# A fused attention and feed-forward kernel: feed-forward products in slots of one bank, vector work in 128x512 pieces

## The chip, the cores and the metric

The kernel runs on one core of one Trainium2 chip. Its time is the device time of one launch in microseconds (us); lower is better. The engines are TensorE (PE in the profile, its weight loads PEld), VectorE (DVE), ScalarE (ACT), GpSimd (POOL) and SyncE (SP), which issues the DMAs.

## The reference

Clustered attention (16 heads of 768 tokens, 64 wide) gives x, 1536 tokens by 512. Two feed-forward blocks follow, and they are what the change is about:

```python
def _moe_ref(x, w_in, w_out):                 # block 1: 512 -> 2048 -> 512
    h = x @ w_in
    g = np.maximum(h, 0.0) + np.log1p(np.exp(-np.abs(h)))
    return (g @ w_out).astype(np.float32)
...
def _moe2_ref(x, w_gate, w_val, w_out):       # block 2: 512 -> 1536 -> 512
    g = x @ w_gate
    silu = g * (1.0 / (1.0 + np.exp(-g)))
    val = x @ w_val
    return (silu * val @ w_out).astype(np.float32)
```

The feed-forward weights come as float64 and are narrowed to float32 on the chip.

## The kernel before

Every float32 product is made of three products of a faster type, float32r: x = hi + lo, and hi x hi, hi x lo and lo x hi are added up in PSUM. So each operand must be split: `hi` is a cast, `lo` a subtraction. The names end in H or h and L or l (XH, XL; gh, gl; whi, wlo).

Attention runs first; its last three steps, `step(N_IT + 1 + n)`, overlap the first projections, and `fin` scales and splits the last pair of heads into XH and XL.

The feed-forward goes by units of 128 hidden columns, 16 in block 1 and 12 in block 2. Tokens are in three chunks of 512. Everything below is one instruction stream per engine, in the order in which the program writes it; PSUM has eight banks of 128x512, handed out in turn.

- `h_unit` (block 1): three banks, one for each chunk; 36 matmuls (four slices of 128 rows, three products, three chunks; the chunk is the innermost loop, so successive matmuls go to different banks, L731). Then ScalarE takes Abs of each bank (L788), VectorE the maximum with 0 (L789). Over all 1536 tokens at once follow Exp (L792) and Ln (L793) on ScalarE, the sum (L796) on VectorE, the cast to gh (L769) on ScalarE and the subtraction to gl (L770) on GpSimd.
- `y_group` (block 1): for two units, the product with w_out into 12 banks of six matmuls (L813), each added to `acc` by VectorE (L827). Units 2g + 2 and 2g + 3 are projected ahead of group g's products.
- `a_unit` and `o_group` (block 2): gate, Sigmoid (L875), product with the gate (L876), values, product (L887), split; then products with w_out2 (L913), added to acc2 (L925) and, in the last group, sent to memory.
- Weights: each 128x512 tile is loaded as float64 bits, narrowed by one ScalarE instruction (L115) and four VectorE instructions (L116, L119, L123, L126), then split by a cast on VectorE (L135, whi) and a subtraction on GpSimd (L136, wlo). These are tasks in a queue `todo`, two for each tile; `pump` emits one or two of them between parts of the products, and `need` emits tasks until a tile that is asked for is there.

Of the kernel before, what the change touches and what calls it, by code (L numbers as in the profile page):

```python
# [11 lines left out]
F32 = mybir.dt.float32  # L12
F32R = mybir.dt.float32r
# [27 lines left out]
def kernel(  # L41
# [60 lines left out]
    def w_narrow(loaded):  # L102
        """float64 bits [p, a, f, 2] (low word, high word) -> float32 [p, a, f], in two steps

        For 2^-126 <= |x| < 2^128 the float32 exponent is the top bit and the low
        seven bits of the eleven; magnitudes below and above are brought to that
        range's ends first."""
        raw, shape, wide = loaded
        if not wide:
            yield  # L110
            yield raw
# [3 lines left out]
        nc.scalar.activation(out=m.bitcast(F32), in_=hi.bitcast(F32), func=AF.Abs)  # L115
        nc.vector.tensor_scalar(  # L116
# [13 lines left out]

    def w_split(x, pool, tag, bufs):
# [13 lines left out]
    # units of the two feed-forward blocks; a unit's own tiles are split three units  # L145
    # ahead, the tile of the output product with the unit
# [14 lines left out]
    # the first tiles of the second block's values have room early on  # L161
# [11 lines left out]
    W = {}  # L173
# [9 lines left out]
    begun = set()  # L183

    def split_tasks(batch):
        """two steps for each tile"""
# [89 lines left out]
    def warm(n):  # L276
        """the tensor engine's clock rises with its use"""
# [6 lines left out]
    # constants  # L284
# [14 lines left out]
    # centroids over their norms; the block diagonal of a pair of heads  # L299
# [4 lines left out]
    # a square root to float32's accuracy: an estimate and a Newton step  # L304
# [80 lines left out]
    def prep_sims(pr, which, spread=True):  # L385
        """spread: between the transposes of a step"""
# [8 lines left out]
    def prep_arg(pr, step):  # L395
        """the one-hot of the first of the largest"""
# [58 lines left out]
    N_IT = NP * 2 * NT  # L455
    CT = 2                  # query tiles to a chunk of P V
# [124 lines left out]
    # the first pair's; its one-hots get 32 partitions to a head, so that they are copied  # L581
    # to their places by the engines
# [26 lines left out]
    # and the start of the second pair's  # L609
# [93 lines left out]
    for i in range(N_IT + 1):  # L703
# [4 lines left out]
        if i in (0, 26):  # L708
            pump(2)
# [4 lines left out]
    # ================= the two feed-forward blocks =================  # L714
# [10 lines left out]
    def proj(xh, xl, w, banks, kks):  # L725
        """banks[c] += (x @ w)^T over the slices kks, for 512 tokens each"""
        hi, lo = w
        for kk in kks:
            for wt, xt, last in ((hi, xh, 0), (hi, xl, 0), (lo, xh, 1)):
                for c in range(NCH):  # L730
                    nc.tensor.matmul(  # L731
                        banks[c],
                        lhsT=wt[:, kk, :],
                        rhs=xt[:, kk, 512 * c:512 * c + 512],
                        start=(kk == 0 and wt is hi and xt is xh),
                        stop=(kk == KD - 1 and last == 1),
                    )

    # the first products start with the pairs of heads that are done
    h0 = [bank() for _ in range(NCH)]  # L740
    w0 = need(W, ("in", 0))
# [24 lines left out]
    def split_g(g, tag):
        gh = gp.tile([128, NTOK], F32R, tag="gh", name=tag + "h")
        gl = gp.tile([128, NTOK], F32R, tag="gl", name=tag + "l")
        nc.scalar.copy(gh, g)  # L769
        nc.gpsimd.tensor_tensor(out=gl, in0=g, in1=_r(gh), op=ALU.subtract)  # L770
        return gh, gl

    # block 1: y^T = softplus(x w_in) w_out
# [3 lines left out]
    def h_unit(f, banks=None):  # L777
        if banks is None:
            banks = [bank() for _ in range(NCH)]
            w = need(W, ("in", f))  # L780
            for half in range(2):
                proj(XH, XL, w, banks, range(2 * half, 2 * half + 2))
                pump()
        e = tp.tile([128, NTOK], F32, tag="e", name="e")
        r = tp.tile([128, NTOK], F32, tag="s", name="r")
        for c in range(NCH):
            cs = slice(512 * c, 512 * c + 512)
            nc.scalar.activation(out=e[:, cs], in_=banks[c], func=AF.Abs)  # L788
            nc.vector.tensor_scalar_max(r[:, cs], banks[c], 0.0)  # L789

        def log_part():
            nc.scalar.activation(out=e, in_=e, func=AF.Exp, scale=-1.0)  # L792
            nc.scalar.activation(out=e, in_=e, func=AF.Ln, bias=1.0)  # L793

        def sum_part():
            nc.vector.tensor_tensor(out=e, in0=r, in1=e, op=ALU.add)  # L796
            g_t[f] = split_g(e, "g")

        return [log_part, sum_part], split_tasks(batches.pop(0))

    def y_group(g):
        last = g == NF1 // 2 - 1
        nd = 1
        for d0 in range(0, KD, nd):
            banks = [bank() for _ in range(nd * NCH)]
            for ff in range(2):
                hi, lo = need(W, ("out", 2 * g + ff))
                gh, gl = need(g_t, 2 * g + ff)
                for d in range(nd):
                    ds_ = slice(128 * (d0 + d), 128 * (d0 + d) + 128)  # L810
                    for n, (wt, gt) in enumerate(((hi, gh), (hi, gl), (lo, gh))):
                        for c in range(NCH):
                            nc.tensor.matmul(  # L813
                                banks[NCH * d + c],
                                lhsT=wt[:, 0, ds_],
                                rhs=gt[:, 512 * c:512 * c + 512],
# [153 lines left out]
```

## Time and profile before

| | us |
|---|---|
| median of 3 runs | 862.71 |
| lowest and highest | 860.93, 866.04 |
| span of the profiled execution | 861.7 |

The profiled execution's span runs from its first to its last instruction; the page gives no other time for it. TensorE is the busiest engine, 95% of the span. Attention takes the first 260 us or so, block 1 runs to about 560 us, block 2 to the end. A row of the trace names line, engine and operation, then what is written and read; "x3" is a count, and "<-" after idle time names what ended it.

### The profile page before, as it was taken

The numbers are of one execution on the slowest core, as the hardware profiler recorded it, in microseconds if no ns is written. First come the engines' busy times: TensorE is split into PE (matmuls) and PEld (weight loads), VectorE is DVE, ScalarE is ACT, GpSimd is POOL, SyncE is SP. The second block draws the span as 40 slices with busy tenths as digits, with TensorE's granted clock in tenths as the row PEclk, the third lists the DMA queues.
The fourth block names the chain that finished last, engine by engine and source line by source line (L and its number), as shares of the span: only waits on it lengthen the run. The fifth ranks groups of instructions, "written<-read, shape, count | busy, mean of one in ns | idle before, by whom it ended". The sixth has DMA issues, their size and how long they took to land.

```text
span 861.7 us, 11737 instructions
## 1 busy us (share of the span) xinstructions
PE 820.9 (95%) x4366; PEld 697.5 (81%) x4366; DVE 683.9 (79%) x1016; ACT 397.6 (46%) x735; POOL 336.0 (39%) x229
## 2 busy tenths in 40 slices
PE   7999999999999999989898997799999999999998
PEld 6899999999898778768777786588888888888886
DVE  6888978988896778898888888849886868876464
ACT  4689889888893755433244433232212212120210
POOL 3636465555522545444244333424433312332110
PEclk9799999999999999999999999999999999999999
DMA  8975775575312132122221120202312221220003
GB/s 200 248 163 134 190 150 142 141 172 122 85 38 69 49 98 74 51 74 80 65 74 50 49 74 25 68 7 74 97 50 74 74 73 49 74 72 26 1 1 146
DMA packets 65336, 75.42 MB, mean 88 GB/s; under 512 B 28960, under 2 KB 51584, under 8 KB 65280
## 3 DMA queue, kind: packets, MB, share of 16 engines
q1 hardware_dynamic: 65280, 74.68, 32.3%
q8 instruction: 34, 0.56, 0.3%
q14 instruction: 22, 0.18, 0.1%
HBM read 48.27 MB, written 3.19 MB: 60 GB/s over the span
## 4 chain that ended last, share of the span: by engine, by line
PE 60%; DVE 25%; DMA 5%; issue 4%; ACT 4%; POOL 1%; SPq 0%; POOLq 0%; ACTq 0%; DVEq 0%
PE bank L731 28%; PE bank L913 11%; PE sps L466 5%; PE ops L515 5%; DVE m L116 5%; PE tps L498 5%; DVE acc L827 5%; DVE e L796 3%; PE bank L813 2%; DVE r L789 2%; DVE m L126 2%; DVE m L123 2%; DMA rd<-rt 2%; DMA R<-rd 2%; DVE whi L135 2%
## 5 line engine op out<-in xcount | busy, mean ns | idle before, releaser
L136 POOL TENSOR_TENSOR wlo<-m,whi 128x512 fp32r<-128x512 f32 x68 | 100.7, 1480 | 291.9 <-DVE whi L135 266.1
L116 DVE TENSOR_SCALAR m<-m 128x512 f32<-128x512 f32 x68 | 86.0, 1265 | 38.4 <-ACT m L115 38.4
L505 DVE TENSOR_TENSOR tl<-tps,th 128x384 fp32r<-128x384 f32 x192 | 98.8, 550 | 20.2 <-ACT th L504 19.6
L474 DVE TENSOR_REDUCE nm<-sps 128x1 f32<-128x768 f32 x96 | 91.3, 952 | 14.3 <-PE sps L466 11.4
L498 PE MATMUL tps<-id,p 128*128 128x128 f32 x576 | 95.3, 282 | 1.1 <-DVE tl L505 1.1
L504 ACT CAST th<-tps 128x384 fp32r<-128x384 f32 x192 | 84.6, 491 | 20.1 <-PE tps L498 17.1
L482 ACT ACTIVATE p<-sps,nm 128x768 f32<-128x768 f32 x96 | 88.1, 918 | 5.6 <-DVE nm L474 5.6
L466 PE MATMUL sps<-KT,QT 128*128 128x384 f32 x384 | 84.7, 343 | 5.6 <-ACT p L482 3.7
L731 PE MATMUL bank<-YH,whi 128*128 128x512 f32 x288 | 81.6, 391 | 2.5 <-DVE acc L827 2.5
L498 PEld LDWEIGHTS tps<-id,p 128*128 128x128 f32 x576 | 76.4, 153 | 8.4 <-DVE tl L505 5.1
L731 PE MATMUL bank<-YL,whi 128*128 128x512 f32 x288 | 81.6, 392 | 0.0
L731 PE MATMUL bank<-YH,wlo 128*128 128x512 f32 x288 | 81.6, 392 | 0.0
L769 ACT CAST gh<-e 128x1536 fp32r<-128x1536 f32 x16 | 23.7, 1481 | 122.8 <-DVE e L796 122.8
L515 PE MATMUL ops<-th,VV 128*128 128x256 f32 x288 | 79.7, 306 | 0.0
L813 PE MATMUL bank<-gh,whi 128*128 128x512 f32 x192 | 58.9, 407 | 17.3 <-DVE r L789 8.2
L115 ACT ACTIVATE m<-raw 128x512 f32<-128x512 f32 x68 | 44.5, 666 | 62.1 <-POOL wlo L136 62.0
L515 PE MATMUL ops<-tl,VV 128*128 128x256 f32 x288 | 71.9, 279 | 0.0
L770 POOL TENSOR_TENSOR gl<-e,gh 128x1536 fp32r<-128x1536 f32 x16 | 57.1, 3573 | 34.5 <-ACT gh L769 30.7
L466 PEld LDWEIGHTS sps<-KT,QT 128*128 128x128 f32 x384 | 63.4, 191 | 6.7 <-ACT p L482 4.4
L731 PEld LDWEIGHTS bank<-YH,whi 128*128 128x128 f32 x288 | 54.4, 189 | 14.3 <-issue 2.9
L731 PEld LDWEIGHTS bank<-YH,wlo 128*128 128x128 f32 x288 | 54.5, 189 | 11.4
L731 PEld LDWEIGHTS bank<-YL,whi 128*128 128x128 f32 x288 | 54.5, 189 | 11.3
(124 smaller groups left out, 1776.6 us busy)
## 6 DMA issues: line engine op xcount, KB each, us to landing
raw<-in_moe_w_out_dram SPq DMA_DIRECT2D x28, 512.0 KB, 3.3
raw<-in_moe_w_in_dram SPq DMA_DIRECT2D x16, 512.0 KB, 3.9
QT<-hi SPq DMA_DIRECT2D x32, 192.0 KB, 3.1
raw<-in_moe_w_val_dram SPq DMA_DIRECT2D x12, 512.0 KB, 4.0
raw<-in_moe_w_gate_dram SPq DMA_DIRECT2D x12, 512.0 KB, 3.5
KT<-hi SPq DMA_DIRECT2D x14, 384.0 KB, 5.8
qn<-in_q_dram SPq DMA_DIRECT2D x16, 192.0 KB, 5.7
kn<-in_k_dram SPq DMA_DIRECT2D x16, 192.0 KB, 4.2
```

The source lines that it names most:

```text
L116: nc.vector.tensor_scalar(out=m.bitcast(F32), in0=m.bitcast(F32), scalar1=F64_LEAST, scalar2=F64_MOST, op0=ALU.max, op1=ALU.min)
L136: nc.gpsimd.tensor_tensor(out=lo, in0=x, in1=_r(hi), op=ALU.subtract)
L466: nc.tensor.matmul(ps[:, c, 0:384], lhsT=Q[:, a, 128 * j:128 * j + 128], rhs=K[:, a, 384 * c:384 * c + 384], start=(a == 0), stop=(a == 1),)
L474: nc.vector.tensor_reduce(out=nm, in_=ps[:, :, 0:384], axis=AX.XY, op=ALU.max, negate=True)
L482: nc.scalar.activation(out=_h(p), in_=s_t.pop(i)[:, :, 0:384], func=AF.Exp, bias=nm_t.pop(i), accum_out=sm_t[pr][:, j:j + 1],)
L498: nc.tensor.transpose(ps[:, 128 * j:128 * j + 128], p[:, 128 * kb:128 * kb + 128], id32)
L504: nc.scalar.copy(th, pv)
L505: nc.vector.tensor_tensor(out=tl, in0=pv, in1=_r(th), op=ALU.subtract)
L515: nc.tensor.matmul(o[:, 0:CW], lhsT=VV_t[pr][:, hh, kb].rearrange("p a d -> p (a d)"), rhs=t[:, kb, :], start=(kb == 0 and lohi == 0), sto ...
L731: nc.tensor.matmul(banks[c], lhsT=wt[:, kk, :], rhs=xt[:, kk, 512 * c:512 * c + 512], start=(kk == 0 and wt is hi and xt is xh), stop=(kk ...
L813: nc.tensor.matmul(banks[NCH * d + c], lhsT=wt[:, 0, ds_], rhs=gt[:, 512 * c:512 * c + 512], start=(ff == 0 and n == 0), stop=(ff == 1 and ...
L913: nc.tensor.matmul(bk, lhsT=lhs[:, ts_], rhs=rhs[:, 0, :], start=(ff == 0 and n == 0), stop=(ff == 1 and n == 2),)
```

## The change

Block 1 and block 2 are written anew as slots. A projection (`proj`) makes the 12 matmuls of one unit and one chunk, one after the other into one bank. `h_slot` follows it with Abs, Exp and Ln over that bank's 128x512 on ScalarE (`soft`), the maximum and the sum in one VectorE instruction that reads the bank and Ln's result, and, one slot later, the split into gh (ScalarE) and gl (GpSimd), again 128x512 each. `y_group` goes by chunk first and then by output rows. In block 2 a gate slot and a value slot alternate, Silu takes the place of Sigmoid and one product, and output products go in pairs of banks. A small calendar (`soon`, `late`, `tick`) puts the vector work of a slot behind it. Weight tiles are split in four tasks of which the first is free, one task a slot (`pump`); after attention their cast whi is on ScalarE (`cast[0]`). A third weight tile is split within attention, and the first three slots (chunk 0 of units 0, 1 and 2) stand in and after attention's last steps, none behind the first of these.

```diff
-        nc.vector.tensor_copy(hi, x)
+        cast[0](hi, x)
         nc.gpsimd.tensor_tensor(out=lo, in0=x, in1=_r(hi), op=ALU.subtract)
...
-        for _ in range(n or (2 if len(todo) > 4 else 1)):
+    def pump(n=1):
+        for _ in range(n):
             if todo:
+                if todo[0] in firsts:
+                    todo.popleft()()
                 todo.popleft()()
+                if todo and todo[0] in firsts:
+                    todo.popleft()()
...
-        if i in (0, 26):
-            pump(2)
+        if i in (0, 26, N_IT - 14):
+            pump(3)
...
+    def proj(xh, xl, w, c):
+        bk = bank()
         hi, lo = w
+        for kk in range(KD):
+            for n, (wt, xt) in enumerate(((hi, xh), (hi, xl), (lo, xh))):
+                nc.tensor.matmul(
+                    bk,
+                    lhsT=wt[:, kk, :],
+                    rhs=xt[:, kk, 512 * c:512 * c + 512],
...
+    cast[0] = nc.scalar.copy
...
+    def soft(f, c, bk):
+        e = tp.tile([128, 512], F32, tag="e", name="e")
+        nc.scalar.activation(out=e, in_=bk, func=AF.Abs)
+        nc.scalar.activation(out=e, in_=e, func=AF.Exp, scale=-1.0)
+        nc.scalar.activation(out=e, in_=e, func=AF.Ln, bias=1.0)
+        def total():
+            nc.vector.scalar_tensor_tensor(out=e, in0=bk, scalar=0.0, in1=e, op0=ALU.max, op1=ALU.add)
+        late[now[0]].append(total)
+        after(1, late, split_g, g_t, f, c, e)
...
+    def h_slot(f, c, n=1):
+        if (f, c) not in hb:
+            hb[f, c] = proj(XH, XL, need(W, ("in", f)), c)
+        after(1, soon, soft, f, c, hb.pop((f, c)))
+        if c == NCH - 1:
+            todo.extend(split_tasks(batches.pop(0)))
+        tick(n)
...
+            nc.scalar.activation(out=sg, in_=bk, func=AF.Silu)
...
+    def o_group(g):
+        for t0 in range(0, NTOK // 128, 2):
...
+            for t, bk in enumerate(bks, t0):
+                after(1, soon, o_sum, g, t, bk)
+            tick()
```

VectorE in the middle of block 1. Before, from one sum over 1536 tokens (L796) to the next:

```order
L796 TENSOR_TENSOR e<-r,e 128x1536
L116 TENSOR_SCALAR m<-m 128x512 [waits Activation_49]
L119 TENSOR_SCALAR m<-m 128x512 [waits DVE_49]
L827 TENSOR_TENSOR acc<-bank,acc 128x512 [waits PE_49] x3
L123 SCALAR_TENSOR_TENSOR m<-raw,m 128x512 [waits DMAHW2_49,DVE_49]
L126 SCALAR_TENSOR_TENSOR m<-raw,m 128x512 [waits DVE_49]
L135 CAST whi<-m 128x512 [waits DVE_49]
```

Now, where the sums into acc end and the slots begin (L812 is the fused maximum and sum, L118 to L128 the weight steps L116 to L126):

```order
L830 TENSOR_TENSOR acc<-bank,acc 128x512
L118 TENSOR_SCALAR m<-m 128x512 [waits Activation_49]
L121 TENSOR_SCALAR m<-m 128x512 [waits DVE_49]
L812 SCALAR_TENSOR_TENSOR e<-bank,e 128x512 [waits Activation_49]
L125 SCALAR_TENSOR_TENSOR m<-raw,m 128x512 [waits DMAHW0_49,DVE_49]
L128 SCALAR_TENSOR_TENSOR m<-raw,m 128x512 [waits DVE_49]
L812 SCALAR_TENSOR_TENSOR e<-bank,e 128x512 [waits Activation_49] x2
```

The cast is gone from VectorE, the maximum and the sum have become L812, and a weight tile's steps stand between pieces of one slot.

TensorE at attention's end (ops are attention's last products, L515 before). Before, three banks in turn behind the first of the last steps:

```order
L515 MATMUL ops<-tl,VV 128x256
L731 MATMUL bank<-XH,whi 128x512 x3
L731 MATMUL bank<-XL,whi 128x512 x3
L731 MATMUL bank<-XH,wlo 128x512 x3
L515 MATMUL ops<-th,VV 128x256 [waits DVE_49]
```

Now, with the tiles' numbers, the same place:

```order
L526 MATMUL ops_3877<-tl_3807,VV_3225 128x256
L526 MATMUL ops_3921<-th_3863,VV_3225 128x256
L526 MATMUL ops_3921<-tl_3864,VV_3225 128x256
L526 MATMUL ops_3921<-th_3863,VV_3225 128x256
L526 MATMUL ops_3921<-tl_3864,VV_3225 128x256
L526 MATMUL ops_3921<-th_3863,VV_3225 128x256
L526 MATMUL ops_3921<-tl_3864,VV_3225 128x256
L742 MATMUL bank_3928<-XH_65,whi_342 128x512
L742 MATMUL bank_3928<-XL_66,whi_342 128x512
L742 MATMUL bank_3928<-XH_65,wlo_343 128x512
L742 MATMUL bank_3928<-XH_65,whi_342 128x512
```

The second group of ops follows the first with no projection between them, and the projection that comes then stays in one bank.

ScalarE around the start of an output group in block 1. Before, late in the block, with the weights' first step L115 as the only step of a weight tile:

```order
L788 ACTIVATE e<-bank 128x512 [waits PE_49] x3
L792 ACTIVATE e<-e 128x1536 [waits Activation_49]
L793 ACTIVATE e<-e 128x1536 [waits Activation_49]
L115 ACTIVATE m<-raw 128x512 [waits DMAHW1_49,Pool_49]
L788 ACTIVATE e<-bank 128x512 [waits PE_49,Pool_49]
```

Now, from the last slot of unit 11 on (L807 to L809 are its Abs, Exp and Ln, L798 the copies gh, L140 the cast whi, L116 the next tile's first step); the first L140 is that of w_out's tile 9, for which the fifth output group asks:

```order
L807 ACTIVATE e<-bank 128x512 [waits PE_49,Pool_49]
L808 ACTIVATE e<-e 128x512 [waits Activation_49]
L809 ACTIVATE e<-e 128x512 [waits Activation_49]
L798 CAST gh<-e 128x512 [waits DVE_49]
L140 CAST whi<-m 128x512 [waits DVE_49]
L116 ACTIVATE m<-raw 128x512 [waits DMAHW6_49,Pool_49]
L798 CAST gh<-e 128x512
```

The cast whi now stands on ScalarE behind a slot's three functions and a copy.

## Rows read from the trace of the kernel before

**Rows 1.** The page's busy times, share of the span, instructions.

```profile
PE 820.9 (95%) x4366; PEld 697.5 (81%) x4366; DVE 683.9 (79%) x1016; ACT 397.6 (46%) x735; POOL 336.0 (39%) x229
```

**Rows 2.** Busy time by engine, two stretches: PE, PEld, DVE, ACT, POOL, PEclk, DMA, GB/s.

```profile
260.00:560.00 300.00, 275.81 (x1174) 220.05 (x1174) 252.81 (x333) 127.11 (x157) 121.94 (x57) 0.99 0.21 64
560.00:860.00 300.00, 297.86 (x1294) 243.65 (x1293) 213.36 (x305) 59.75 (x87) 83.13 (x45) 0.99 0.18 59
```

**Rows 3.** Who TensorE waited for, 259 to 560 us: total, times, longest.

```profile
PE bank L813 <- DVE r L789: 8.2, 5, 3.8
PE bank L813 <- DVE acc L827: 7.9, 5, 2.4
```

**Rows 4.** In order of time near 415 us: start, us, engine, instruction, idle before.

```profile
414.40 3.50 POOL L770 TENSOR_TENSOR gl<-e,gh 128x1536 fp32r<-128x1536 f32 x1 [5.40 <-ACT gh L769]
...
414.91 3.27 DVE L116 TENSOR_SCALAR m<-m 128x512 f32<-128x512 f32 x1 [2.10 <-ACT m L115]
...
419.30 0.60 PE L813 MATMUL bank<-gh,whi 128*128 128x512 f32 x1 [2.39 <-DVE acc L827]
```

**Rows 5.** Busy time by engine, one stretch; the granted clock is 0.93.

```profile
420.00:440.00 20.00, 20.00 (x83) 16.36 (x83) 17.55 (x24) 6.84 (x8) 8.87 (x4) 0.93 0.25 80
```

**Rows 6.** Single lines, 260 to 862 us: duration in ns, least/median/most, first, last.

```profile
L116 DVE TENSOR_SCALAR m<-m x66: 412/420/3346, 270.5 to 832.2; 128x512 f32<-128x512 f32 x66
...
L119 DVE TENSOR_SCALAR m<-m x66: 426/428/3614, 271.0 to 832.6; 128x512 int32<-128x512 int32 x66
...
L126 DVE SCALAR_TENSOR_TENSOR m<-raw,m x66: 691/692/1670, 272.2 to 836.8; 128x512 int32<-128x512 int32 x66
...
L136 POOL TENSOR_TENSOR wlo<-m,whi x66: 1269/1303/2663, 273.4 to 838.2; 128x512 fp32r<-128x512 f32 x66
```

**Rows 7.** Groups by line, 260 to 560 us: busy, mean ns of one; idle before.

```profile
L136 POOL TENSOR_TENSOR wlo<-m,whi 128x512 fp32r<-128x512 f32 x36 | 58.4, 1621 | 138.1 <-DVE whi L135 120.6 <-PE bank L813 14.6 <-PE bank L731 2.9
...
L770 POOL TENSOR_TENSOR gl<-e,gh 128x1536 fp32r<-128x1536 f32 x16 | 57.1, 3573 | 34.5 <-ACT gh L769 30.7 <-issue 3.8
...
L116 DVE TENSOR_SCALAR m<-m 128x512 f32<-128x512 f32 x36 | 53.1, 1476 | 27.5 <-ACT m L115 27.5
...
L827 DVE TENSOR_TENSOR acc<-bank,acc 128x512 f32<-128x512 f32 x79 | 49.6, 679 | 0.2 <-PE bank L813 0.2
...
L789 DVE TENSOR_SCALAR r<-bank 128x512 f32<-128x512 f32 x48 | 30.0, 680 | 6.1 <-ACT e L788 6.1
...
L796 DVE TENSOR_TENSOR e<-r,e 128x1536 f32<-128x1536 f32 x16 | 29.0, 1817 | 0.1
...
L788 ACT ACTIVATE e<-bank 128x512 f32<-128x512 f32 x48 | 25.0, 595 | 10.8 <-PE bank L731 9.0 <-POOL gl L770 1.9
...
L115 ACT ACTIVATE m<-raw 128x512 f32<-128x512 f32 x36 | 23.5, 665 | 7.6 <-POOL wlo L136 7.6
...
L829 ACT CAST YH<-acc 128x512 fp32r<-128x512 f32 x7 | 4.3, 621 | 21.7 <-DVE acc L827 21.7
```

**Rows 8.** The chain that ended last: start, us, engine, line, count.

```profile
266.32 20.43 PE bank L731 x90
...
403.34 3.75 PE bank L813 x16
...
559.62 66.66 PE bank L731 x286
...
626.28 16.81 PE bank L913 x72
...
855.80 2.79 DVE acc L925 x4
```

**Rows 9.** In order of time, attention's end: start, us, engine, instruction, idle before.

```profile
260.33 1.02 DVE L505 TENSOR_TENSOR tl<-tps,th 128x384 fp32r<-128x384 f32 x2 [0.57 <-ACT th L504]
...
260.65 0.84 PE L731 MATMUL bank<-XH,whi 128*128 128x512 f32 x3
...
269.41 0.51 ACT L577 CAST XH<-xu 128x384 fp32r<-128x384 f32 x1 [1.09 <-DVE xu L575]
```

More of the change, by code (lines that the diff above doesn't have):

```diff
@@ L129, in w_narrow @@
         yield m.bitcast(F32)
+    cast = [nc.vector.tensor_copy]
     def w_split(x, pool, tag, bufs):
@@ L723, in bank, with tick, after @@
         return pool.tile([128, 512], F32, tag="b", name="bank")
-    def proj(xh, xl, w, banks, kks):
+    def proj(xh, xl, w, c):
+        bk = bank()
         hi, lo = w
[L728 to L741, printed above, removed]
+        for kk in range(KD):
[4 more added lines that the diff above has]
+                    rhs=xt[:, kk, 512 * c:512 * c + 512],
+                    start=(kk == 0 and n == 0),
+                    stop=(kk == KD - 1 and n == 2),
+                )
+        return bk
+    cast[0] = nc.scalar.copy
+    soon, late = collections.defaultdict(list), collections.defaultdict(list)
+    now = [0]
+    def tick(n=1):
+        now[0] += 1
+        for f in soon.pop(now[0], []):
+            f()
+        pump(n)
+        for f in late.pop(now[0], []):
+            f()
+    def after(lag, table, f, *a):
+        table[now[0] + lag].append(functools.partial(f, *a))
+    hb = {}
     for n in range(3):
         step(N_IT + 1 + n)
-        proj(XH, XL, w0, h0, range(n, n + 1))
+        if n:
+            hb[n - 1, 0] = proj(XH, XL, need(W, ("in", n - 1)), 0)
     assert not events, events
+    hb[2, 0] = proj(XH, XL, need(W, ("in", 2)), 0)
     pctx.close()
@@ L762, with cols @@
     gp = ctx.enter_context(tc.tile_pool(name="gp", bufs=4, reuse_waits="tile"))
-    tp = ctx.enter_context(tc.tile_pool(name="tp", bufs=2, reuse_waits="tile"))
+    tp = ctx.enter_context(tc.tile_pool(name="tp", bufs=4, reuse_waits="tile"))
     pool_of["c"] = (mp, 3)
[L766 to L771, printed above, removed]
+    def cols(c):
+        return slice(512 * c, 512 * c + 512)
@@ L774, with split_g @@
+    def split_g(table, f, c, g):
+        if f not in table:
+            table[f] = [gp.tile([128, NTOK], F32R, tag=t, name=t) for t in ("gh", "gl")]
+        gh, gl = table[f]
+        nc.scalar.copy(gh[:, cols(c)], g)
+        nc.gpsimd.tensor_tensor(out=gl[:, cols(c)], in0=g, in1=_r(gh)[:, cols(c)], op=ALU.subtract)
     acc = mp.tile([128, KD, NTOK], F32, tag="acc", name="acc")
     g_t = {}
[L777 to L799, printed above, removed]
@@ L801, in y_group, with y_sum @@
+    def y_sum(g, d, c, bk):
+        a = acc[:, d, cols(c)]
+        if g == 0:
+            nc.scalar.copy(a, bk)
+        else:
+            nc.vector.tensor_tensor(out=a, in0=bk, in1=a, op=ALU.add)
+        if g == NF1 // 2 - 1:
+            nc.scalar.copy(YH[:, d, cols(c)], a)
+            eng = nc.gpsimd if c < NCH - 1 else nc.vector
+            eng.tensor_tensor(out=YL[:, d, cols(c)], in0=a, in1=_r(YH)[:, d, cols(c)], op=ALU.subtract)
     def y_group(g):
-        last = g == NF1 // 2 - 1
@@ L803, in y_group @@
-        nd = 1
-        for d0 in range(0, KD, nd):
-            banks = [bank() for _ in range(nd * NCH)]
+        for n in range(KD * NCH):
+            c, d = divmod(n, KD)
+            bk = bank()
             for ff in range(2):
                 hi, lo = need(W, ("out", 2 * g + ff))
[L808 to L816, printed above, removed]
-                                start=(ff == 0 and n == 0),
-                                stop=(ff == 1 and n == 2),
-                            )
-            for n, bk in enumerate(banks):
-                d, c = d0 + n // NCH, n % NCH
-                cs = slice(512 * c, 512 * c + 512)
-                a = acc[:, d, cs]
-                if g == 0:
-                    nc.scalar.copy(a, bk)
-                else:
-                    nc.vector.tensor_tensor(out=a, in0=bk, in1=a, op=ALU.add)
-                if last:
-                    nc.scalar.copy(YH[:, d, cs], a)
-                    eng = nc.gpsimd if c == 1 or c == 2 and d < KD - 1 else nc.vector
-                    eng.tensor_tensor(out=YL[:, d, cs], in0=a, in1=_r(YH)[:, d, cs], op=ALU.subtract)
-            pump()
@@ new lines, in a_slots, with silu, product @@
+    def a_slots(f, c):
+        bk = proj(YH, YL, need(W, ("gate", f)), c)
+        sg = tp.tile([128, 512], F32, tag="e", name="sg")
+        def silu(bk=bk):
+            nc.scalar.activation(out=sg, in_=bk, func=AF.Silu)
+        after(1, soon, silu)
+        tick()
+        bk = proj(YH, YL, need(W, ("val", f)), c)
+        def product():
+            nc.vector.tensor_tensor(out=sg, in0=bk, in1=sg, op=ALU.mult)
+            after(1, soon, split_g, a_t, f, c, sg)
+        after(1, soon, product)
+        if c == NCH - 1 and batches:
+            todo.extend(split_tasks(batches.pop(0)))
+        tick()
@@ L904, in o_group, with o_sum @@
+    def o_sum(g, t, bk):
+        a = acc2[:, t, :]
+        if g == 0:
+            nc.vector.tensor_copy(a, bk)
+        else:
+            nc.vector.tensor_tensor(out=a, in0=bk, in1=a, op=ALU.add)
+        if g == NF2 // 2 - 1:
+            nc.sync.dma_start(out=outv[t // NT, t % NT], in_=a)
     def o_group(g):
-        for t0 in range(0, NTOK // 128, 4):
-            bks = [bank() for _ in range(4)]
+        for t0 in range(0, NTOK // 128, 2):
+            bks = [bank() for _ in range(2)]
```

139 lines of the change are left out of this document (48 added, 91 removed).

## The prediction

> **What bounds the kernel now.** I read the busy shares first, then the two blocks of the feed-forward by windows, then who TensorE waited for, then one such wait in order of time. TensorE is busy 95% of the span [rows 1], but not evenly: between 260 and 560 us, block 1 (softplus), it is busy 275.81 of 300 us, between 560 and 860 us, block 2, 297.86 [rows 2]. So block 2 is bound by its matmuls, and what the change does to vector work there is worth nothing unless it makes TensorE wait; block 1 has 24.2 us of waits. The longest are for VectorE, for the maximum (L789) and the sum into acc (L827), which empty the banks [rows 3]. [rows 4] show one: GpSimd's 128x1536 subtraction gl (L770) begins at 414.40 and takes 3.50 us; VectorE's L116 begins at 414.91 and ends 0.3 us behind it, after 3.27 us, where its median is 0.420 [rows 6]. The bank sums stand behind it on VectorE, and TensorE waits 2.39 us. Over 420 to 440 us the granted clock is then 0.93 [rows 5], so for a part of that stretch the lower level (1.2 GHz): 0.07 x 20 = 1.4 us for such a drop. VectorE is busy 252.81 of 300 us [rows 2], of which L116 has 53.1 where 36 x 0.420 = 15.1 would do [rows 6, 7]: 38.0 us are spent blocked.
>
> The Trainium skill (SBUF — State Buffer, section Who interferes with whom) says that GpSimd and a VectorE instruction in a two-port mode exclude each other for a whole instruction; L116 agrees. It says the same of VectorE instructions with two SBUF inputs, which would make L126 a victim too; L126's median is 0.692 and its longest 1.670, so here this happens seldom.
>
> **The floor of block 1.** It has 576 projection matmuls and 576 output matmuls. Unhindered one takes 20.43 / 90 = 0.227 and 3.75 / 16 = 0.234 us [rows 8]: 130.8 + 134.8 = 265.6 us. From the first projection at 260.65 [rows 9] to block 2's first at 559.62 [rows 8] it takes 299.0 now.
>
> **VectorE in block 1, for a unit of 128 hidden columns.** Now: two weight tiles of 0.420 + 0.428 + 0.692 (the unshown L123 taken as L126, same shape) + 0.692 and the cast (taken as L119, 0.428), 5.3; six sums of 0.679, 4.1; three maxima of 0.680 and one sum of 1.817, 3.9 [rows 6, 7]; 38.0 / 16 = 2.4 of blocking: 15.7 of TensorE's 265.6 / 16 = 16.6, with waits on top. After: the cast goes to ScalarE, -0.9. The fused step has one PSUM and one SBUF operand like L827, so 3 x 0.68 = 2.0 for the 3.9. That leaves 10.6. The blocking lies between 0 and all of GpSimd's work, five 128x512 pieces a unit of 1.303 (L136) = 6.5 us; I take the share of now, 38.0 of the 58.4 + 57.1 us that L136 and L770 ran, a third: 2.1, in all 12.7. VectorE no longer sets the pace, and one block lasts 1.3 us, not 3.5.
>
> **ScalarE in block 1.** Abs 0.595, and Exp, Ln and the copy gh 0.621 each (L829, the same shape) make 2.46 a slot; a weight tile 0.665 + 0.621 for the new cast = 1.29 [rows 7]. A unit: 3 x 2.46 + 2 x 1.29 = 10.0 of 16.6. Within the six slots of a pair of units it is 14.8 + 2.6 = 17.4 against 72 x 0.227 = 16.3 for TensorE; eight banks cover the lag of 1.1, and in the 12 output banks that follow (16.8 us, two tiles or 2.6 of ScalarE) it is made up.
>
> **Where TensorE will still wait.** (1) The first of attention's last three steps has no projection behind it now; the next needs tl, begun at 260.33 and 1.02 long [rows 9]: 0.8 us. Those steps' own matmuls cost 1.4, as before. (2) The first output group. ScalarE turns to the slots after its last copy to XH, at 269.9 [rows 9]: 12 x 1.84 + 11 copies x 0.62 + 6.5 tiles x 1.29 = 37.3, so to 307.2, the fused step behind it to 307.9. The eighth output bank reuses the twelfth slot's, and TensorE is there at 260.65 + 0.8 + 1.4 + 12 x 2.72 + 7 x 1.40 = 305.4: 2.5, ends 0 and 5. (3) Two weight tiles, w_out's 9 and 15, aren't finished when the output product asks. For tile 9 the order on ScalarE shows it: behind the three functions of unit 11's last slot stands a copy gh and only then the cast whi; on GpSimd gl stands before wlo. From the end of that slot: 1.84 + 0.62 + 0.62 = 3.1 to whi, asked for at 0.7: 2.4; wlo at 2.5 + 2 x 1.3 = 5.1, asked for at 3.1 + 0.5: 1.5. Together 3.9. For tile 15 VectorE's four steps, 2.2, stand behind a sum of 0.7, then 0.62 and 1.3, so whi at 3.5 and wlo at 4.8: 2.8 + 0.8, or 3.7 unrounded. (4) Each of these two lets the clock drop: 2 x 1.4 = 2.8.
>
> Sum: 265.6 + 1.4 + 0.8 + 2.5 + 3.9 + 3.7 + 2.8 = 280.7, which is 18.3 under 299.0. The step to block 2 costs nothing: the last output group goes by chunks of tokens, so 8 banks (11 us) lie between the last sum of chunk 0 and the gate slot that reads it; without that cover a sum, a copy and a subtraction would stand there, 0.68 + 0.62 + 1.3 = 2.6.
>
> **Small terms.** A third weight tile within attention: VectorE 2.7 with its cast, of which I take 0.5 (ends 0 and 2.7). The end: two banks are finished together there, so two sums of 2.79 / 4 = 0.7 [rows 8] stand behind the last matmul, the first begun a matmul early, where one stood: +0.4. Silu, the dropped product, the smaller pieces, the paired banks in block 2: nothing, under its matmuls; VectorE has 300 - 213.36 = 87 us to spare there [rows 2], and only past that would they cost. The program has as many table loads as before. The weights' loads keep their number and their three buffers, at a DMA share of 0.21 [rows 2].
>
> **Twelve matmuls to one bank.** The trace has no projection that adds twelve times to one bank. In L913 two of three successions stay in a bank, at 16.81 / 72 = 0.2335; L813 changes it every time and takes 0.234 [rows 8]. So the 7 ns over 0.227 go with the operands, not with the bank, and I take 0.227. The ends: the output products sink to 0.227 too, 1008 x 6.5 ns = -6.6; the projections rise to 0.2335, 1440 x 6.5 ns = +9.4.
>
> **The sum.** 861.7 - 18.3 + 0.5 + 0.4 = 844.3 us of span. The median of the runs, 862.71, is 1.0 above the span of before: **845.3 us**. Half a per cent, 4.3 us, is what a measurement of this kernel can tell from no change.
>
> **Rivals.** (A) The forecast, 838 to 852 by the ends of its terms: 0.58. (B) No waits: the 12.9 us of (2) to (4) go, 832.4: 0.10. For it: eight banks, three spare tiles; against it: the order at tile 9. (C) The vector engines still set the pace in block 1: VectorE is blocked for all of GpSimd's 6.5, 10.6 + 6.5 = 17.1 a unit, (17.1 - 16.6) x 16 = 8 us more, 853.3; with ScalarE's 1.1 in each of six pairs not made up, 859.9: 0.16, of which 0.03 for the latter. The skill's rule on two SBUF inputs would bring this case, as GpSimd's pieces are more now; L126's median speaks against. (D) The other side: successive additions to one bank delay each other. Its place is the 1440 projections, its price 1.44 us for each ns. At 0.2335 a matmul it gives 854.7 (0.05); from (17.4 + 4.3) / 1440 = 15 ns on, 0.242 a matmul, the kernel is slower than before, 871.2 at 0.245 (0.07); between them 0.04. For it: no run of twelve is in the trace; against it: L913. That the work doesn't keep a slot behind, as the change says, is (3), and counted.
>
> **Chances.** Faster by over 0.5%: 0.58 + 0.10 + 0.13 + 0.05 = 0.86; within: 0.03 + 0.04 = 0.07; slower: 0.07. The range 832 to 858 leaves out C's upper end and D's upper two cases.
>
> **What would show it.** Block 1: its stretch from the first projection to block 2's first gate lasts 281 us; L116 (now L118) means under 0.9 us and never over 1.8; TensorE waits about 4 us twice, for a cast whi and a subtraction wlo, and nowhere over 1 us for acc. Projections keep 0.227; more means D. If the fused step or ScalarE ends a wait of TensorE in most pairs, it is C. If block 2 takes over 300 us, its cover is gone and I am wrong there.

## The result and the profile after

The changed kernel takes 872.17 us (median of 4 runs, 870.06 to 875.1) and the kernel before, on the same chip, 863.38 (860.93 to 866.04). The ratio is 1.010, 95% interval 1.0072 to 1.0129: **slower by 1%**, where 845.3 was predicted. The profiled execution takes 872.08 us, its span is 870.3.

The busy line of the page of after, which answers to [rows 1]:

```profile
PE 825.1 (95%) x4366; PEld 702.2 (81%) x4366; DVE 566.7 (65%) x895; ACT 458.6 (53%) x918; POOL 345.2 (40%) x287
```

VectorE is relieved as meant, from 79% to 65%, and TensorE is as busy as before, 95%, in a longer span. The chain that ended last of after (start, us, what), as [rows 8]:

```profile
271.20 2.72 PE bank L742 x12
...
332.48 16.33 PE bank L742 x72
348.81 16.86 PE bank L845 x72
...
569.14 65.28 PE bank L742 x288
```

The timeline shows the first projection (the chain has it 0.2 us later):

```profile
268.89 0.28 PE L526 MATMUL ops<-tl,VV 128*128 128x256 f32 x1
270.22 0.39 PE L526 MATMUL ops<-th,VV 128*128 128x256 f32 x1 [1.05 <-DVE xu L547]
...
271.03 0.39 PE L742 MATMUL bank<-XH,whi 128*128 128x512 f32 x1
```

It comes at 271.03 where it came at 260.65 [rows 9], 10.4 us later. But it also stands one step of attention later in the order than before: the 2.0 us from 269.0 on, a wait of 1.05 us and the matmuls of that step, lie ahead of it now, and the prediction counts them in block 1. So attention itself has lost 8.4 us. From its first projection block 1 takes 298 us up to block 2's first gate at 569.14; with the 2.0 us it is 300, where it took 299.0: the 18.3 us that were to be gained there are not there. Block 2 lasts as long as before, 301.2 to the end against 302.1, and TensorE waits for nothing in it. What TensorE waited for in after (us in total, times, longest), to be held against [rows 3]:

```profile
PE bank L845 <- ACT whi L140: 11.2, 3, 5.8
PE sps L477 <- ACT p L493: 10.1, 2, 9.0
PE bank L742 <- ACT whi L140: 4.5, 1, 4.5
PE bank L845 <- DVE e L812: 3.0, 1, 3.0
PE tps L509 <- DVE tl L516: 2.7, 4, 1.3
...
PE bank L845 <- POOL wlo L141: 0.8, 2, 0.6
```

The waits for sums and maxima of [rows 3] are gone. In block 1 TensorE now waits for weight tiles: 11.2 + 4.5 + 0.8 us, with the 3.0 for the first output group 19.5. In attention its longest wait is 9.0 us, for the exponential (p). And the clock falls oftener; the windows of after in block 1 whose granted clock is under 0.95 (busy times of PE, PEld, DVE, ACT, POOL, then the granted clock, DMA share, GB/s), as [rows 5]:

```profile
300.00:320.00 20.00, 18.98 (x70) 14.80 (x71) 14.83 (x20) 14.21 (x25) 10.36 (x8) 0.83 0.29 85
...
440.00:460.00 20.00, 14.03 (x52) 10.66 (x51) 12.62 (x13) 13.39 (x24) 11.89 (x9) 0.84 0.17 52
...
480.00:500.00 20.00, 17.50 (x69) 13.65 (x69) 11.08 (x15) 14.14 (x25) 10.45 (x8) 0.91 0.17 52
...
540.00:560.00 20.00, 16.28 (x57) 12.22 (x56) 12.36 (x22) 4.23 (x7) 5.77 (x5) 0.83 0.18 54
```

20 x (0.17 + 0.16 + 0.09 + 0.17) = 11.8 us, at most: the clock can fall shortly before a wait ends, and that part costs nothing. Floor 265.6 + the last step's matmuls 0.7 + waits 19.5 + clock 11.8 = 297.6 accounts for block 1's 298.

**Two of these waits in order of time.** The timeline of after where TensorE asks for the weight tile of w_in's unit 3, called in 3 here (start, us, engine, line; in brackets the idle time before and what ended it):

```profile
295.68 0.63 ACT L809 ACTIVATE e<-e 128x512 f32<-128x512 f32 x1
296.22 0.64 ACT L116 ACTIVATE m<-raw 128x512 f32<-128x512 f32 x1
296.89 0.43 DVE L118 TENSOR_SCALAR m<-m 128x512 f32<-128x512 f32 x1 [2.12 <-ACT m L116]
...
297.82 1.64 DVE L125 SCALAR_TENSOR_TENSOR m<-raw,m 128x512 int32<-128x512 int32 x1
...
300.21 0.62 ACT L140 CAST whi<-m 128x512 fp32r<-128x512 f32 x1 [1.03 <-DVE m L128]
...
300.88 0.80 PE L742 MATMUL bank<-XH,whi 128*128 128x512 f32 x1 [4.49 <-ACT whi L140]
```

TensorE ran out at 296.4, and the tile's first step (Abs, L116) began at 296.22, behind a softplus function on ScalarE; VectorE had been idle 2.12 us for it. And w_out's tile 9, out 9:

```profile
448.50 0.66 ACT L116 ACTIVATE m<-raw 128x512 f32<-128x512 f32 x1
448.74 1.28 POOL L141 TENSOR_TENSOR wlo<-m,whi 128x512 fp32r<-128x512 f32 x1 [1.15 <-ACT whi L140]
...
449.19 1.11 DVE L118 TENSOR_SCALAR m<-m 128x512 f32<-128x512 f32 x1 [0.31 <-ACT m L116]
...
449.98 1.45 POOL L799 TENSOR_TENSOR gl<-e,gh 128x512 fp32r<-128x512 f32 x1
...
450.34 1.38 DVE L121 TENSOR_SCALAR m<-m 128x512 int32<-128x512 int32 x1
...
452.07 1.26 POOL L799 TENSOR_TENSOR gl<-e,gh 128x512 fp32r<-128x512 f32 x1 [0.64 <-ACT gh L798]
452.24 1.64 DVE L125 SCALAR_TENSOR_TENSOR m<-raw,m 128x512 int32<-128x512 int32 x1
453.92 0.69 DVE L128 SCALAR_TENSOR_TENSOR m<-raw,m 128x512 int32<-128x512 int32 x1
454.64 0.62 ACT L140 CAST whi<-m 128x512 fp32r<-128x512 f32 x1 [2.65 <-DVE m L128]
```

The whole tile is made within the 6.8 us before its use (PE follows at 455.31, after 5.83 us). Three of VectorE's four steps take 1.11, 1.38 and 1.64 us where unblocked ones take 0.43, 0.43 and 0.68: each overlaps a piece of GpSimd, wlo (L141) or gl (L799). So a tile seems to be late because its steps are handed out late, at one task a slot, and most of them then take long; the runs below test that.

**Attention's start.** The timeline of after where the 9.0 us wait ends:

```profile
26.93 0.66 ACT L116 ACTIVATE m<-raw 128x512 f32<-128x512 f32 x1 [8.32 <-DMA raw<-in_moe_w_in_dram]
27.62 0.90 ACT L493 ACTIVATE p<-sps,nm 128x768 f32<-128x768 f32 x1
...
28.66 1.65 PE L477 MATMUL sps<-KT,QT 128*128 128x384 f32 x4 [8.95 <-ACT p L493]
```

At step 0 the new `pump` hands out a tile's three tasks and then also the next tile's free first one. That one is an Abs on ScalarE, whose data come by DMA only at 26.9; attention's exponential stands behind it, and TensorE behind that.

### The profile page after: what moved, and what is told of

The parts are those of the page before. It is cut to its first block, busy times and chain, and to the rows that moved or that the text cites. A ratio compares the mean times of both kernels' runs of the same rounds, so it can differ in the third digit from the quotient of the medians.

```text
span 870.3 us, 11899 instructions
## 1 busy us (share of the span) xinstructions
PE 825.1 (95%) x4366; PEld 702.2 (81%) x4366; DVE 566.7 (65%) x895; ACT 458.6 (53%) x918; POOL 345.2 (40%) x287
## 4 chain that ended last, share of the span: by engine, by line
PE 78%; ACT 7%; DVE 7%; DMA 3%; issue 2%; SPq 1%; POOL 1%; DVEq 0%; POOLq 0%; ACTq 0%
PE bank L742 31%; PE bank L845 15%; PE bank L910 12%; PE tps L509 6%; PE ops L526 6%; PE sps L477 6%; PE sims L388 2%; ACT e L808 1%; DVE m L125 1%; ACT e L807 1%; DVE tl L516 1%; DVE m L118 1%; PE mps L351 1%; DVE m L128 1%; DMA R<-rd 1%
## 5 line engine op out<-in xcount | busy, mean ns | idle before, releaser
L141 POOL TENSOR_TENSOR wlo<-m,whi 128x512 fp32r<-128x512 f32 x68 | 88.0, 1294 | 232.5 <-ACT whi L140 150.2
L742 PE MATMUL bank<-YL,whi 128*128 128x512 f32 x288 | 112.1, 389 | 0.0
L742 PE MATMUL bank<-YH,whi 128*128 128x512 f32 x288 | 112.1, 389 | 0.0
L140 ACT CAST whi<-m 128x512 fp32r<-128x512 f32 x65 | 40.0, 616 | 136.7 <-DVE m L128 136.7
L516 DVE TENSOR_TENSOR tl<-tps,th 128x384 fp32r<-128x384 f32 x192 | 99.0, 551 | 18.9 <-ACT th L515 18.5
L485 DVE TENSOR_REDUCE nm<-sps 128x1 f32<-128x768 f32 x96 | 91.5, 953 | 21.3 <-PE sps L477 18.7
L515 ACT CAST th<-tps 128x384 fp32r<-128x384 f32 x192 | 85.0, 492 | 23.2 <-PE tps L509 20.3
L845 PE MATMUL bank<-gh,whi 128*128 128x512 f32 x192 | 79.3, 413 | 14.2 <-ACT whi L140 11.2
L799 POOL TENSOR_TENSOR gl<-sg,gh 128x512 fp32r<-128x512 f32 x36 | 50.9, 1415 | 94.5 <-ACT gh L798 94.5
L799 POOL TENSOR_TENSOR gl<-e,gh 128x512 fp32r<-128x512 f32 x48 | 67.6, 1413 | 33.3 <-ACT gh L798 23.1
L742 PE MATMUL bank<-XH,whi 128*128 128x512 f32 x192 | 76.0, 396 | 4.5 <-ACT whi L140 4.5
L845 PE MATMUL bank<-gh,wlo 128*128 128x512 f32 x192 | 79.0, 411 | 1.0 <-POOL wlo L141 0.8
L830 DVE TENSOR_TENSOR acc<-bank,acc 128x512 f32<-128x512 f32 x84 | 55.9, 685 | 36.2 <-PE bank L845 36.1
L845 PE MATMUL bank<-gl,whi 128*128 128x512 f32 x192 | 78.3, 408 | 0.0
L742 PE MATMUL bank<-XH,wlo 128*128 128x512 f32 x192 | 75.8, 395 | 0.1
```

The costliest lines, as they stand in the source:

```text
L485: nc.vector.tensor_reduce(out=nm, in_=ps[:, :, 0:384], axis=AX.XY, op=ALU.max, negate=True)
L515: nc.scalar.copy(th, pv)
L516: nc.vector.tensor_tensor(out=tl, in0=pv, in1=_r(th), op=ALU.subtract)
L742: nc.tensor.matmul(bk, lhsT=wt[:, kk, :], rhs=xt[:, kk, 512 * c:512 * c + 512], start=(kk == 0 and n == 0), stop=(kk == KD - 1 and n == 2),)
L799: nc.gpsimd.tensor_tensor(out=gl[:, cols(c)], in0=g, in1=_r(gh)[:, cols(c)], op=ALU.subtract)
L845: nc.tensor.matmul(bk, lhsT=wt[:, 0, ds_], rhs=gt[:, cols(c)], start=(ff == 0 and j == 0), stop=(ff == 1 and j == 2),)
```

## The experiments

My theory: (a) the early Abs costs attention some 6 us; (b) late tiles cost block 1 the rest. The rivals stand with each run. A row gives the median, the ratio to the kernel before on the same chip with its interval, and, by the chain of the profile, attention's end (start of the first projection) and block 1 (from there to block 2's first gate, in the kernel before behind its wait of 2.5 us). In before, e3 and e4 the first projection stands a step of attention earlier: against the other rows add 2.0 to their attention's end and take 2.0 from their block 1.

| run | median us | ratio | attention's end | block 1 |
|---|---|---|---|---|
| before | 863.38 | 1 | 260.8 | 298.8 |
| after | 872.17 | 1.010 [1.0072, 1.0129] | 271.2 | 297.9 |
| e1_no_front_abs | 867.55 | 1.0044 [1.0029, 1.0059] | 265.8 | 298.9 |
| e2_tiles_early | 853.08 | 0.9867 [0.9828, 0.9907] | 273.9 | 278.2 |
| e3_before_front_abs | 870.92 | 1.0085 [1.0063, 1.0107] | 266.3 | 300.2 |
| e4_before_gl3 | 854.44 | 0.9896 [0.9867, 0.9926] | 263.9 | 290.9 |
| e5_spread | 868.38 | 1.0054 [1.0032, 1.0076] | 264.2 | 299.9 |
| e6_spread_tiles | 847.77 | 0.9808 [0.9772, 0.9843] | 265.7 | 279.0 |
| e7_order | 849.05 | 0.9829 [0.98, 0.9859] | 270.3 | 278.8 |
| e8_cast_on_vector | 864.74 | 0.9999 [0.9982, 1.0015] | 272.3 | 289.3 |
| e9_rest_on_vector | 868.07 | 1.0057 [1.0027, 1.0088] | 274.7 | 292.3 |
| e10_tiles_and_cast | 842.67 | 0.976 [0.973, 0.979] | 267.9 | 274.8 |
| e11_tiles_cast_order | 845.25 | 0.9803 [0.9784, 0.9822] | 266.5 | 275.3 |
| e12_tiles_cast_rest | 845.75 | 0.9811 [0.9772, 0.985] | 269.0 | 277.9 |

### No early Abs, and the early Abs alone

```diff
 # e1, on after
-            pump(3)
+            for _ in range(4):
+                todo.popleft()()
 # e3, on before
-            pump(2)
+            pump(3 if i == 0 else 1)
```

> The changed kernel, but within attention each of the three weight tiles is split in exactly four tasks, without the Abs of the following tile that the new pump emits behind them. Theory T1 (ScalarE's Abs stands ahead of attention's first exponential and waits there for its tile's load): the 9.0 us wait of TensorE near 20 us goes, the later loss near 235 us stays: 872.2 - 6 = 866. Rival R1 (the whole tile in one burst, or the third tile, is what delays attention): no change, 871 to 873.

> The kernel before, with one thing of the change alone: at attention's first step the Abs of the second weight tile is emitted behind the first tile's two tasks. T1: 863.4 + 6 = 869, and ScalarE waits some 8 us for the load of raw ahead of the first exponential. R1: no change, 862 to 865.

Both ways it is the Abs: taking it away (e1, at all three tiles) gains 4.6 us, and putting it alone into the kernel before (e3, at the first) costs 7.4. TensorE's waits for the exponential, first in e1, then in e3:

```profile
PE sps L477 <- ACT p L493: 2.4, 2, 1.4
```

```profile
PE sps L466 <- ACT p L482: 9.4, 2, 8.5
```

### Tiles handed out earlier

```diff
 # e2, on after: y_group
-                tick()
+                tick(2)
```

> The changed kernel, but two weight-tile tasks instead of one in every slot of the first block's output products, so that no tile is unfinished when it is asked for. Theory T2 (TensorE's waits in block 1 are tiles that come too late, each followed by a stretch at the lower clock): the waits near 450, 492 and 546 us go, 5.8 + 2.5 + 3.7 = 12.0, and 8.5 us of lower clock with them: 872.2 - 20 = 852; the waits near 296 and 322 us stay. Rival R2 (ScalarE, VectorE and GpSimd together are too slow for block 1, so that the waits only move): 869 to 875.

19 us for one figure. The same instructions are issued; only the tasks come earlier in the order. What is left of TensorE's waits in block 1 in e2, but for one of 0.4 us:

```profile
PE bank L742 <- ACT whi L140: 4.5, 1, 4.5
PE bank L845 <- DVE e L812: 3.2, 1, 3.2
```

The 11.2 us for w_out's tiles are gone, and with them all clock drops of block 1 but the one after in 3. The wait for in 3 lies before the first output group, where nothing was changed, and stays at 4.5. Of the 19.7 us by which block 1 is shorter, 11.4 are waits and some 8.4 go with the clock, which falls once now (3.4 us) where it fell four times.

### The pieces alone, in the kernel before

```diff
 # e4, on before
-        nc.gpsimd.tensor_tensor(out=gl, in0=g, in1=_r(gh), op=ALU.subtract)
+        for c in range(NCH):
+            cs = slice(512 * c, 512 * c + 512)
+            nc.gpsimd.tensor_tensor(out=gl[:, cs], in0=g[:, cs], in1=_r(gh)[:, cs], op=ALU.subtract)
```

> The kernel before, with GpSimd's subtraction gl of block 1 in three pieces of 128x512 and nothing else. Theory T3 (one 3.5 us subtraction that holds VectorE's L116 is what makes TensorE wait in the kernel before): L116 is never over 1.8 us, TensorE's waits in block 1 fall from 24 to some 12 us, 863.4 - 10 = 853. Rival R3 (the blocking is GpSimd's total time, which only grows, and VectorE's own work sets the pace): within 3 us of 863.

So the reading of [rows 4] was right: GpSimd's long subtraction made the bank sums late, and cutting it in three is worth 1% by itself. In block 1 L116's longest falls from 3.29 to 1.58 us, and block 1 from 298.8 to 290.9.

### The third tile spread over attention

```diff
 # e5, on after
-        if i in (0, 26, N_IT - 14):
-            pump(3)
+        if i in (0, 26):
+            for _ in range(4):
+                todo.popleft()()
+        if i in (42, 48, 54, 60):
+            todo.popleft()()
 # e6: and tick(2) in y_group
```

> The changed kernel; in attention the tasks of a tile are handed out so that no free first is pulled ahead at step 0, and the third tile's four tasks go one at a time to steps 42, 48, 54 and 60 in place of all at step 82. Theory: attention's loss against the kernel before (10.4 us) is these two bursts, so nearly all but the new tail (about 1 us) comes back: 872.2 less 8 to 9 = 863 to 864, with the first projection near 262. Rival: the third tile costs VectorE's place in attention wherever it stands; then as in the run without the early free first, 867.5.

> The same, and in the feed-forward's output groups two tasks are handed out at a step instead of one, so that the weight tiles are finished earlier. Theory: the two losses lie in different stages and add: 853.1 less 8 to 9 = 844 to 845, which is the prediction's own floor with its clock drops. Rival: block 1 starting earlier finds its tiles as much later, and the gains don't add: 850 or more.

e5 is no faster than e1 (1.0054 against 1.0044): my theory of two bursts falls by half. Spread out, the third tile brings TensorE 5.3 us of waits for tl (L516) where after has 2.7. VectorE has little room in attention: 16.5 to 18.7 us busy of each 20 from 60 us on. In e1 the tile's burst is followed by a wait of 2.3 us for tl and a stretch with the clock at 0.57 (230 to 238 us), which e5 does not have. What the tile costs is not shown. By e1's profile the first projection comes 265.6 - 260.65 = 4.9 later than before, of which 2.0 are its later place in the order: 2.9 for the tile; by e5's it would be 1.4. And e4, whose attention is that of the kernel before, ends it 3.1 us later than that kernel's profile. A version without the third tile was not tried. e6 lies 5.3 below e2, as e1 lies 4.6 below after: the two losses add, but to 848, not to the 844 that I expected of all of attention's loss.

### Another order of the first slots

```diff
 # e7, on e6
-    for f, c in ((0, 0), (1, 0), (2, 0), (0, 1), (1, 1), (0, 2), (1, 2), ...
+    for f, c in ((0, 0), (1, 0), (2, 0), (0, 1), (0, 2), (1, 1), (1, 2), ...
```

> The same, and the first slots of block 1 run in an order that ends with a weight tile one slot earlier, so that the tile in 3 gets its buffers earlier. Theory: the wait for in 3 (4.5 us in the run with two tasks a step) is a wait for buffers and falls by about one slot's 2.7 us, and the clock drop behind it (up to 3.4 us) with it: 839 to 842. Rival: the tile is late because VectorE and GpSimd can't make it faster: no change against the run before this one, 845.

The time is the rival's, but its reason is not: the wait for in 3 does fall, from 4.5 to 2.3, only the time doesn't. TensorE's waits in e7, and its windows:

```profile
PE bank L848 <- DVE e L815: 4.1, 1, 4.1
PE bank L745 <- ACT whi L140: 2.3, 1, 2.3
```

```profile
290.00:310.00 20.00, 17.60 (x64) 13.48 (x63) 11.65 (x16) 17.43 (x31) 11.95 (x9) 0.83 0.22 70
310.00:330.00 20.00, 15.89 (x60) 12.40 (x59) 16.46 (x19) 12.52 (x23) 10.75 (x8) 0.83 0.29 90
```

The next wait grew by 0.5 (3.6 in e6), I take it because ScalarE is late by the same work, which no run separates; and the clock falls twice by 0.17 x 20 = 3.4 us, where in e6 the second fall cost 1.8 (0.91 in the same window). The shorter wait cost a whole fall all the same.

### The cast of weight tiles back on VectorE

```diff
 # e8, on after
-    cast[0] = nc.scalar.copy
 # e9, on e8: wlo on VectorE too, from block 1 on
-        nc.gpsimd.tensor_tensor(out=lo, in0=x, in1=_r(hi), op=ALU.subtract)
+        rest[0].tensor_tensor(out=lo, in0=x, in1=_r(hi), op=ALU.subtract)
```

> The changed kernel with the last cast of a weight tile left on VectorE after attention, in place of ScalarE. Theory: tiles are late because their VectorE steps are handed out late, and the cast's engine matters by no more than its queue: within 3 us of 872.2. Rival: the cast waits in ScalarE's queue behind the softplus functions and makes the tiles late: 5 us or more faster.

> The changed kernel with both the weight cast and the weight rest (the subtraction that makes wlo) on VectorE from block 1 on, in place of ScalarE and GpSimd. To be held against the run with the cast alone on VectorE, 864.7. Theory: VectorE's steps of a late tile are slow because GpSimd's pieces block them (out 9's two last steps took 1.69 us instead of 0.68), and wlo is the smaller half of GpSimd's work in block 1 (35 pieces of 1.29 against 48 of 1.41 us); with it gone, and with wlo 0.6 us shorter, tiles are finished earlier: 858 to 862. Rival: VectorE pays 0.69 us for each wlo and stays blocked by the other pieces: 863 to 868.

Here my theory fell: e8 is 7.4 us faster than after, so the cast's engine matters too. The timeline of e8 at in 3:

```profile
295.19 0.64 ACT L116 ACTIVATE m<-raw 128x512 f32<-128x512 f32 x1
...
299.69 0.42 DVE L140 CAST whi<-m 128x512 fp32r<-128x512 f32 x1
...
300.17 0.50 PE L742 MATMUL bank<-XH,whi 128*128 128x512 f32 x1 [2.62 <-DVE whi L140]
```

TensorE ran out at 297.55 here and the Abs began 2.36 us before that; in after it began 0.17 before. Every cast that ScalarE doesn't make (0.62 us) brings the next tile's Abs and the next softplus functions forward, since one queue serves all three. The wait for in 3 falls from 4.5 to 2.6 (and 0.7 for wlo), the one at the first output group from 3.0 to 1.1. Only 0.6 us less is waited for out 9, as the theory had it. Of the 8.6 us by which block 1 is shorter than in after, only 3.6 are waits; some 4.8 go with the clock, whose drops come to 7.0 us by the windows in place of 11.8.

e9's rival holds: 3.3 us slower than e8. The blocked time of VectorE doesn't fall with the 45 us of GpSimd work that went: by the means of its weight steps over their unblocked times it is 35 x (0.20 + 0.29 + 0.34 + 0.14 + 0.24 + 0.03) = 43 us in e9 and 35 x (0.13 + 0.34 + 0.41 + 0.11 + 0.14) = 40 in e8. The gl pieces that are left block it as long in sum.

### Together

```diff
 # e10: e6, and the cast stays on VectorE
-    cast[0] = nc.scalar.copy
 # e11: e10 with e7's order; e12: e10 with e9's wlo on VectorE
```

> The spread attention tiles, two tasks a step in the output groups, and the cast on VectorE. Theory: with two tasks a step out 9, 11 and 15 are early whatever the cast's engine, so of the cast's 7.4 us only its part at the first slots remains: in 3's wait 4.5 becomes 3.3, the wait at the first output group 3.6 becomes about 1.5, and one clock drop of 1.8 us goes: 842 to 844. Rival: the cast gained by making late tiles earlier and by nothing else, and those are early here: 847 to 849.

> The same with block 1's first slots in the order that ends with a weight tile one slot earlier. Theory: in the earlier run of that order the wait for in 3 fell by 2.2 us but a second clock drop and a longer wait at the output group took it back; without the casts in ScalarE's queue that wait is gone and 2 to 4 us are gained on the run before this one: 839 to 841. Rival: no change against it.

> As the run with spread tiles, two tasks a step and the cast on VectorE, with wlo on VectorE too. Theory: the last step of in 3 is shorter by 0.6 us and VectorE is blocked less: 1 to 2 us faster than that run. Rival: VectorE becomes the engine that finishes tiles and sums late: 2 us or more slower.

e10 beats both kernels, by 2.4% the one before. Its chain, and TensorE's waits in block 1:

```profile
267.89 2.72 PE bank L745 x12
...
542.71 65.28 PE bank L745 x288
```

```profile
PE bank L847 <- DVE e L814: 2.7, 1, 2.7
PE bank L745 <- DVE whi L140: 2.6, 1, 2.6
...
PE bank L745 <- POOL wlo L141: 0.7, 1, 0.7
```

Block 1 takes 274.8 us, 9 over its floor. e11 and e12 add nothing: in e11 the wait for in 3 is down to 1.1 and the one at the output group is up to 5.0, which I read as the same ScalarE lag in another place; in e12, where VectorE makes wlo too, the wait for in 3 is 4.6 again.

## Why the prediction was wrong

**What held.** Block 1 is now limited by its matmuls and a few waits, the bank sums no longer set the pace; rival D falls: projections of twelve additions to one bank run at 16.33 / 72 = 0.227 us in the chain above, as taken. The first output group waits 2.96 where 2.5 was worked out, the tile out 15 3.5 + 0.2 where 3.7 was, attention's tail 1.05 where 0.8 was. VectorE's own sum was right too: it is busy 199 us in block 1, 12.5 a unit, where 12.7 was worked out. Block 2 is unchanged; the sign set for it, over 300 us, was set too low, since the kernel before takes 302.1 already. (The 559.62 from which that is counted is block 2's third matmul, behind a wait of 2.5 us; after has no wait there, as was said.) L118 means 0.727 us with 1.125 at most, within the bounds set; VectorE is blocked for 39 us in all, where 2.1 x 16 = 34 were taken.

**Failed: the small term for attention.** 0.5 us with ends 0 and 2.7; measured 8.4, the 10.4 less the 2.0 that the prediction has in block 1. Its price counted VectorE's work for a third tile and left out what else `pump(3)` hands out: the diff shows the "first" task taken behind a tile as well as ahead of it, and I called it free. e1 puts it at 4.6 us, e3 at 7.4. The prediction reasons from queues twice (the bank sums behind L116, the cast whi behind a slot's functions) and didn't do so here. What the third tile itself cost, 2.9 us by e1's profile and 1.4 by e5's, is open.

**Failed: (3), which tiles are late, and by how much.** Two tiles at 3.9 and 3.7 stood there. The runs show four: in 3 (4.5) and out 11 (1.9 + 0.6) weren't in it, and out 9 took 5.8. For out 9 I let whi follow 3.1 us behind the slot's end by ScalarE's order alone; in the trace the tile's own VectorE steps end last, three of the four blocked by GpSimd, and whi is done 6.5 us behind the slot's end. I spread the blocking evenly (12.7 of 16.6 us a unit) and held that enough; this late tile meets it at three steps of four. Of in 3 I priced VectorE's and ScalarE's work in sum, not the place of its Abs behind the softplus functions. e2 shows that the order in which tasks are handed out decides this, e8 that ScalarE's queue does too.

**Failed: (4), the price of a clock drop.** 2.8 us for two; measured up to 11.8 for four. The 1.4 came from the one drop in [rows 5]. After the waits of 3.5, 4.5 and 5.8 us the stretch at the lower clock was 7 us long, not 3.

Of the 26.0 us between the span worked out, 844.3, and the one measured, 870.3, attention makes 8.4 - 0.5 = 7.9, the weight tiles 16.5 - 7.6 = 8.9 and the clock up to 11.8 - 2.8 = 9.0.

**The two-input rule.** I used the median of L126 to set aside what the Trainium skill says (SBUF — State Buffer, section Who interferes with whom) of VectorE instructions with two SBUF inputs: that they contend with a GpSimd instruction that reads SBUF. The groups of after in block 1 decide for the rule (idle time behind the second bar):

```profile
L125 DVE SCALAR_TENSOR_TENSOR m<-raw,m 128x512 int32<-128x512 int32 x35 | 33.6, 959 | 0.2
...
L121 DVE TENSOR_SCALAR m<-m 128x512 int32<-128x512 int32 x35 | 29.6, 845 | 1.2
L128 DVE SCALAR_TENSOR_TENSOR m<-raw,m 128x512 int32<-128x512 int32 x35 | 28.1, 802 | 1.2
L118 DVE TENSOR_SCALAR m<-m 128x512 f32<-128x512 f32 x35 | 25.5, 727 | 17.1 <-ACT m L116 17.1
```

L125 means 0.959 against 0.68 unblocked. Before, the same step (L123) meant 0.687 in block 1, so it rarely met GpSimd; I take it that the order kept the bank sums between, which no run tests. It didn't bring case C, the vector engines as the pace: VectorE is busy 199 of block 1's 298 us.

The forecast's slower side held D alone, 0.07. The case that came, tiles and attention late by order, had no chance of its own: "a slot behind" was counted as true but for two tiles. The gain itself was there to be had: with tasks handed out in time block 1 takes 278.2 us (e2), or 280.2 counted as the prediction counts it, where 280.7 was predicted. That they are so near is in part luck, as the waits left in e2 (in 3, the first output group) are not the ones in the sum.

**Open.** Attention's code is the same in e5, e6, e7, e10, e11 and e12, yet its end in their profiles lies between 264.2 and 270.3. The clock goes with it: by windows of 10 us the stretches at the lower level come to 3.4 to 5.2 us lost in e5, e6 and e11, which end it by 266.5, and to 8.6 in e7, e10 and e12, which end it from 267.9 on. What makes the clock fall oftener in these wasn't tried. With so much spread, a difference of 2 or 3 us between e10, e11 and e12 rests on the medians alone.

## What to carry to other kernels

Before an instruction is called free because its engine is idle, look at what stands behind it in that engine's queue and at when its data come: one Abs that waits for a DMA cost 5 to 7 us (e1, e3). When vector work is taken off the critical path, the next thing to be late is what feeds the matmuls, here the weight tiles, and how many tasks a slot hands out can be worth more (19 us) than the rewriting itself. A wait of TensorE must be priced with the clock drop that may follow it: in after none behind 3.0 us, and up to 3.4 us behind 3.5.

## What was not expected of the hardware

The clock drops of block 1 in after come in two sizes, and the length of the wait alone does not tell which, or whether there is one. The windows of 2 us of after behind the wait for in 3 (columns as above):

```profile
298.00:300.00 2.00, 0.00 (x0) 0.00 (x0) 1.97 (x2) 1.16 (x2) 0.91 (x1) 0.99 0.00 0
300.00:302.00 2.00, 1.11 (x2) 0.50 (x2) 1.35 (x3) 1.79 (x4) 1.09 (x1) 0.50 0.37 80
...
306.00:308.00 2.00, 2.00 (x9) 1.58 (x8) 0.42 (x1) 1.97 (x4) 1.45 (x2) 0.80 0.46 112
308.00:310.00 2.00, 2.00 (x11) 1.63 (x10) 0.57 (x2) 1.97 (x5) 1.15 (x2) 1.00 0.43 151
```

It is at the lower level from 300 to 307 us and about as long from 454 and from 549 us (waits of 4.5, 5.8 and 3.5 us), each up to 3.4 us of time; after the 1.9 and 0.6 us waits near 494 it is low for half as long, 1.8 us. In e7 a wait of 2.3 us is followed by the long kind; in after one of 3.0 us, at 325, by none. So a wait made shorter gave back its own time, but not surely its drop.

VectorE's weight steps with one SBUF input (L118, L121) and with two (L125) are both delayed by GpSimd's 128x512 pieces, by up to 1.0 us: 1.41 us at most for L121 against 0.43, 1.72 for L125 against 0.68. Taking 45 of GpSimd's 124 us in block 1 away (e9) didn't lower the sum of these delays.
